# A decode kernel on one Trainium2 core: two product rows turned into columns by a matrix product instead of a trip through DRAM

## The chip, the core and the metric

The kernel runs on one core of one Trainium2 chip. The metric is the device time of one execution in microseconds (us); smaller is better. Before the change it is 402.88 us, the median of three runs (402.80, 402.88, 402.97). Beside these there is one profiled execution, on which all views of the trace rest.

## The reference, cut to what matters

One token is decoded (batch 1, sequence length 1, model width D = 1024). Its layer norm feeds two branches, whose results are added:

```python
x = A_x
xn = _layernorm(x)
return x + _A_ref(xn, A_k_cache, A_v_cache, A_wq, A_wo) + _B_ref(xn, B_w1, B_w2, B_w3, B_w4)

# _A_ref: 32 query heads, 4 key/value heads, 65536 keys of 128 values each
q = (x @ wq) ...; o = softmax(q k^T / sqrt(128)) v; return o @ wo

# _B_ref
h  = gelu(layernorm(x) @ w1)           # 1024 values
hs = concatenate([g0, g1, g2, g3]) @ w2   # g: quarters of h, each shifted along the sequence
x1 = x + hs
return x1 + gelu(layernorm(x1) @ w3) @ w4  # w3: 1024 x 3584, w4: 3584 x 1024
```

Everything is bfloat16. The sequence has one position, so each shifted quarter of `h` is a row of padding: `hs` is zero, and `x1` equals `x`. That is why the kernel can compute `layernorm(x) @ w3` early, before w1 and w2. The caches are 64 MiB each, the weights together about 34 MB; nothing is read twice.

## The kernel before, in words

**Transfers.** All large inputs go through three buffers of 64 KB per partition (tile `slot`, pool `big`, `SLOTS = 3`). The list `slots` (lines 104 to 115) gives the order: wq, K and V of the first half of key/value head 0, w3, K and V of its second half, then K and V in turn for the other heads (each transfer covers 32768 keys, 8.4 MB), with w1 and the first 13 of w4's 28 column pieces in one buffer after head 2, then wo, and last w2 with the rest of w4. `issue` (line 120) puts a load on SP's queue at line 126. A load waits until its buffer is free, so load i waits for the last reader of load i - 3, and SP issues strictly in this order.

**Attention.** `compute_K` (line 360) works on 16384 keys: VectorE transposes 32x32 blocks of K in place (line 369, eight times for each 8.4 MB load), TensorE multiplies with the query (line 373, tile `sc`), VectorE takes the maximum (377, 381, 383, 391 or 393), ScalarE the exponential (396), VectorE transposes the result into `pT` (410). `compute_V` (413) multiplies `pT` with V (420, tile `oacc`), and VectorE or ScalarE moves the result to `og` (425, 428). `group_end` (433) closes a head.

**The small layers.** `rows_product` (line 261) leaves a product with a weight matrix as rows: for w3 the 3584 results lie on partitions 0, 32, 64 and 96, in two blocks of 448 columns; the other 31 partitions of each group of 32 hold zeros, since the left operand `xpad2` has one column that is not zero. ScalarE applies the gelu (line 321, tile `hrow`; line 329, tile `h1row`). The next products, with w4 (line 348) and w2 (341), need the values as columns: `hT` with 28 values on each partition, `gT` with 8. They are used through `row_acc` (line 180), which accumulates in `psB`; only the last piece of w4 reads `psB` out and stores the result (355 to 358).

**From row to column.** `bounce` (line 310) makes the columns. GpSimd's queue (POOL) stores the rows in a DRAM scratch tensor (line 312) and, when that has landed, loads them back with the other layout (line 314, tiles `dst_h` and `dst_g`). Since all sources of `gT` are padding, `grow` is only a memset (331) and the four copies in the loop at 334 to 337 are never issued.

**What sets the order around the change.** The code is written in the order of the loads (line 476). The framework lays the instructions out on each engine: an instruction may stand ahead of one written earlier when its inputs are ready earlier, and each engine then runs its list in order. Tiles with one tag share a pool's buffers. `pT`, `psel`, `accx`, `grow` and the final `out0` share the tag "pT" with two buffers (pool `tpool`); `qrow`, `p_sb`, `hrow` and `h1row` share the tag "p" with one (`ppool`); all small PSUM tiles share the tag "pm" with two (`ps_M`). A tile waits until the earlier user of its buffer is done.

Of the kernel before, what the change touches and what calls it, by code (L numbers as in the profile page):

```python
# [8 lines left out]
BF16 = mybir.dt.bfloat16  # L9
F32 = mybir.dt.float32  # L10
ACTF = mybir.ActivationFunctionType
ALU = mybir.AluOpType
AX = mybir.AxisListType
# [11 lines left out]
def kernel(  # L25
# [14 lines left out]
    nc = tc.nc  # L40
    P = 128
# [8 lines left out]
    DC = D // P  # L50
    FC = F // P
# [9 lines left out]
    const = ctx.enter_context(tc.tile_pool(name="const", bufs=1))  # L61
    small = ctx.enter_context(tc.tile_pool(name="small", bufs=2))
    one = ctx.enter_context(tc.tile_pool(name="one", bufs=1))
    big = ctx.enter_context(tc.tile_pool(name="big", bufs=SLOTS))
    ppool = ctx.enter_context(tc.tile_pool(name="pp", bufs=1))
    tpool = ctx.enter_context(tc.tile_pool(name="tp", bufs=2))
    dram = ctx.enter_context(tc.tile_pool(name="dram", bufs=1, space=bass.MemoryType.DRAM))
    ps_S = ctx.enter_context(tc.tile_pool(name="psS", bufs=2, space=bass.MemoryType.PSUM))
    ps_O = ctx.enter_context(tc.tile_pool(name="psO", bufs=1, space=bass.MemoryType.PSUM))
    ps_M = ctx.enter_context(tc.tile_pool(name="psM", bufs=2, space=bass.MemoryType.PSUM))  # L70
# [46 lines left out]
    st = {}  # L117
# [18 lines left out]
    for a in range(4):  # L136
        nc.scalar.dma_start(out=x_bf[32 * a:32 * a + 32, :],
                            in_=A_x[0, 0, 32 * a * DC:(32 * a + 32) * DC].rearrange("(p c) -> p c", c=DC))
# [16 lines left out]
    ident_f = const.tile([P, P], F32, name="ident_f")  # L155
# [9 lines left out]
    def tmp(w):  # L165
        n_tmp[0] += w
        assert n_tmp[0] <= 512
        return early[:, n_tmp[0] - w:n_tmp[0]]
# [52 lines left out]
    for j in range(4):  # L221
# [6 lines left out]
    sel32 = tmp(32)  # L228
# [5 lines left out]
    nc.vector.tensor_tensor(out=sel8[:], in0=sel8[:], in1=sel32[:, 16:24], op=ALU.add)  # L234
    nc.vector.tensor_tensor(out=sel8[:], in0=sel8[:], in1=sel32[:, 24:32], op=ALU.add)

    maskq = const.tile([P, 4], F32, name="maskq")
    nc.vector.tensor_tensor(out=maskq[:], in0=sel8[:, 0:4], in1=sel8[:, 4:8], op=ALU.add)

# [4 lines left out]
                          in_=sel8[:].unsqueeze(2).to_broadcast([P, 8, 4]))  # L244

    selw = const.tile([P, 2], F32, name="selw")
    for b in range(2):
        nc.vector.tensor_tensor(out=selw[:, b:b + 1], in0=ident_f[:, 32 * b:32 * b + 1],
                                in1=ident_f[:, 64 + 32 * b:64 + 32 * b + 1], op=ALU.add)
# [5 lines left out]
    for b in range(2):  # L255
        for par in range(2):
            nc.vector.tensor_copy(out=psel[:, 2 * b + par, :].rearrange("p (a i) -> p a i", a=4),
                                  in_=iv[:, b, par, :].unsqueeze(1).to_broadcast([P, 4, 32]))


    def rows_product(key, part, wt, xp, width, n_chunks):
        if part == 0:
            st[key] = ps_S.tile([P, 2, 512], F32, name="rows", tag="sc")
        acc = st[key]
        n_c = wt.shape[1]
        for cl in range(n_c):
            c = n_c * part + cl
            for j in range(4):
                for bk in range(2):
                    ch = 4 * bk + j  # L270
                    if ch < n_chunks:
                        nc.tensor.matmul(acc[32 * j:32 * j + 32, bk, 0:width], lhsT=xp[:, c, :],  # L272
                                         rhs=wt[:, cl, ch * width:(ch + 1) * width],
                                         start=(c == 0), stop=(c == DC - 1), tile_position=(0, 32 * j),
                                         skip_group_check=True)
        return acc
# [30 lines left out]
                             skip_group_check=True)  # L307
        nc.vector.tensor_copy(out=qsel[:], in_=pq[:])

    def bounce(rows_ap, view, C, tag):  # L310
        scr = dram.tile([P, C], BF16, name=f"scr_{tag}")
        nc.gpsimd.dma_start(out=view(scr[:].rearrange("m c -> (m c)")), in_=rows_ap)
        dst = const.tile([P, C], BF16, name=f"dst_{tag}")
        nc.gpsimd.dma_start(out=dst[:], in_=scr[:])
        return dst

    def compute_w3():
        wt = loaded[("w3",)].rearrange("p (c n) -> p c n", n=F)
        acc = rows_product("psh", 0, wt, xpad2, FW, 8)
        hrow = ppool.tile([P, 2, FW], BF16, name="hrow", tag="p")  # L320
        nc.scalar.activation(out=hrow[:], in_=acc[:, :, 0:FW], func=ACTF.Gelu_apprx_tanh)
        st["hT"] = bounce(hrow[:].rearrange("(j u) b n -> j u b n", u=32)[:, 0],
                          lambda f: f.rearrange("(b j n) -> j b n", b=2, j=4), FC, "h")

    def compute_w1():
        wt = loaded[("w1",)].rearrange("p (c n) -> p c n", n=D)
        acc = rows_product("psh1", 0, wt, xpad2, 512, 2)
        h1row = ppool.tile([64, 512], BF16, name="h1row", tag="p")
        nc.scalar.activation(out=h1row[:], in_=acc[0:64, 0, :], func=ACTF.Gelu_apprx_tanh)
        grow = tpool.tile([64, 512], BF16, name="grow", tag="pT")  # L330
        nc.vector.memset(grow[:], 0.0)
        cq = D // 4
        for grp, shift in enumerate((1, -1, 2, -2)):
            for s in range(S):
                if 0 <= s - shift < S:
                    r0, c0 = 32 * (grp // 2), cq * (grp % 2)
                    nc.vector.tensor_copy(out=grow[r0:r0 + 1, c0:c0 + cq], in_=h1row[r0:r0 + 1, c0:c0 + cq])
        st["gT"] = bounce(grow[:].rearrange("(j u) n -> j u n", u=32)[:, 0],
                          lambda f: f.rearrange("(j n) -> j n", j=2), DC, "g")

    def compute_w2():
        wt = loaded[("w2",)].rearrange("p (c n) -> p c n", n=D)
# [125 lines left out]
    def add_wo():  # L468
        wrow = st.pop("wrow")
        for q in range(4):  # L470
            c0 = QC * (q % 2)
            row_acc(q, selw[:, q // 2:q // 2 + 1], wrow[:, c0:c0 + QC])

    compute = {"wq": compute_wq, "w3": compute_w3, "w1": compute_w1, "w2": compute_w2, "w4": compute_w4,
               "wo": compute_wo, "K": compute_K, "V": compute_V}
    for i, pieces in enumerate(slots):
# [37 lines left out]
```

## Time and profile before

| | |
|---|---|
| median of three runs | 402.88 us |
| time of the profiled execution | 402.64 us |
| its span, first to last instruction | 400.9 us |
| mean granted TensorE clock | 0.806 |
| TensorE (PE) busy | 217.9 us, 54% |
| VectorE (DVE) busy | 215.1 us, 54% |
| ScalarE (ACT) busy | 35.1 us, 9% |
| GpSimd (POOL) busy | 6.0 us, 1% |
| moved by DMA | 170.10 MB, mean 424 GB/s |

The profiled execution lies 0.24 us under the median, and 1.74 us of its time lie outside the span. "Busy" is the time in which an engine runs an instruction; a matmul's end is modelled, and matmuls overlap. The profile also names, for each group of instructions, the line, the tiles (`out<-in`), the shape, the number, the busy time and the mean time of one, and what ended the idle time before it. The chain of waits goes back from the last instruction to whatever released each step. "us to landing" is the time from a transfer's issue until its data have arrived.

### The profile page before, as it was taken

Reading aid. Unit: us, or ns where it says so; the run is one execution under the profiler, and the core shown is the slowest. Engines: PE = TensorE matmul, PEld = TensorE weight load, DVE = VectorE, ACT = ScalarE, POOL = GpSimd, SP = SyncE. Lnnn points to the kernel's source line nnn. Section 1 sums busy time; section 2 is a strip of 40 time slices with the busy share of each in tenths; the row PEclk is TensorE's granted clock in tenths of the full one; section 3 lists DMA queues with packets and bytes.
Section 4 is the critical chain, followed back from the end, with each engine's and each line's share of the span. In section 5 each row is a group of like instructions: output and inputs, shape, how many; then the busy total and the mean of one; then the engine's idle time right before and its main releaser. Section 6 shows DMA issues by size and latency. Waiting matters only on the chain.

```text
span 400.9 us, 3446 instructions
## 1 busy us (share of the span) xinstructions
PE 217.9 (54%) x1484; PEld 89.7 (22%) x1484; DVE 215.1 (54%) x249; ACT 35.1 (9%) x61; POOL 6.0 (1%) x17
## 2 busy tenths in 40 slices
PE   0006597420976396419563955486803952395773
PEld 0002232210332132104231321132401320132321
DVE  0005398401985598339846962696405962596400
ACT  0001001400012001100110011002100031002000
POOL 3000000000000000000000000000000000000000
PEclk9999879975796589958985996599765998598557
DMA  9999999999999999999999999999999999999994
GB/s 399 438 419 419 419 421 452 452 439 419 425 432 420 419 484 420 432 425 438 420 419 477 420 425 438 439 420 399 466 440 438 419 420 458 438 419 453 402 400 194
DMA packets 4088, 170.10 MB, mean 424 GB/s; under 512 B 735, under 2 KB 745, under 8 KB 1002
## 3 DMA queue, kind: packets, MB, share of 16 engines
q1 hardware_dynamic: 3752, 169.87, 98.2%
q8 instruction: 11, 0.18, 0.2%
q0 software_dynamic: 128, 0.02, 0.0%
q10 hardware_dynamic: 194, 0.00, 0.0%
q14 instruction: 3, 0.02, 0.0%
HBM read 169.88 MB, written 0.01 MB: 424 GB/s over the span
## 4 chain that ended last, share of the span: by engine, by line
DMA 51%; DVE 33%; PE 10%; another core or an unknown queue 3%; ACT 1%; issue 1%; ACTq 0%; SPq 0%; DVEq 0%
DMA slot<-in_A_k_cache_dram 37%; DVE slot L369 27%; DMA slot<-in_B_w_dram 7%; DMA x_bf<-in_A_x_dram 7%; PE oacc L420 4%; PE sc L373 3%; DVE mx L377 3%; PE rows L272 2%; DVE pT L410 1%; PE psB L181 1%; ACT p_sb L396 1%; DVE qst L285 0%; PE pm_mx L386 0%; DVE m L381 0%
## 5 line engine op out<-in xcount | busy, mean ns | idle before, releaser
L373 PE MATMUL sc<-slot,qst 128*128 128x512 bf16 x512 | 134.1, 412 | 101.2 <-DVE slot L369 101.0
L369 DVE STREAM_TRANSPOSE slot<-slot 128x2048 f32<-128x2048 f32 x64 | 142.9, 2280 | 65.7 <-DMA slot<-in_A_k_cache_dram 65.6
L373 PEld LDWEIGHTS <-qst 128*128 128x128 bf16 x512 | 51.5, 103 | 172.0 <-issue 49.5
L420 PE MATMUL oacc<-slot,pT 128*32 128x512 bf16 x512 | 43.8, 503 | 6.4 <-DVE pT L410 3.0
L396 ACT ACTIVATE p_sb<-sc,nm 128x1024 bf16<-128x1024 f32 x16 | 17.8, 1114 | 185.0 <-DVE nm L393 121.1
L410 DVE STREAM_TRANSPOSE pT<-p_sb 128x1024 bf16<-128x1024 bf16 x16 | 19.9, 1245 | 17.3 <-ACT p_sb L396 17.3
L420 PEld LDWEIGHTS <-pT 128*32 128x32 bf16 x512 | 16.0, 118 | 26.4 <-issue 16.3
L428 DVE SCALAR_TENSOR_TENSOR og<-og,alpha,oacc 128x512 f32<-128x512 f32 x12 | 9.0, 747 | 24.2 <-PE oacc L420 24.0
L377 DVE TENSOR_REDUCE mx<-sc 128x1 f32<-128x1024 f32 x16 | 19.3, 1204 | 4.5 <-PE sc L373 4.4
L193 PE MATMUL pm_ln<-early 128*128 128x1 f32 x4 | 1.1, 354 | 33.0 <-DVE early L229 30.5
L187 DVE CAST early<-x_bf 128x8 f32<-128x8 bf16 x1 | 0.2, 172 | 28.9 <-DMA x_bf<-in_A_x_dram 28.9
L379 PE MATMUL pm_mx<-ident_f,mx 128*1 128x128 f32 x16 | 4.5, 281 | 15.9 <-DVE mx L377 15.9
L396 ACT ACT_TABLE_LOAD x3 | 3.8, 1283 | 92.3 <-DVE nm L391 57.3
L443 PE MATMUL pm_e<-og,sel8q 128*32 128x128 f32 x32 | 6.0, 348 | 5.2 <-DVE og L435 5.2
L193 PEld LDWEIGHTS pm_ln<-early 128*128 128x128 f32 x4 | 1.0, 310 | 33.1 <-issue 30.5
L386 PE MATMUL pm_mx<-ident_f,rep 1*128 1x1 f32 x16 | 3.7, 229 | 8.2 <-DVE rep L383 8.2
L463 PE MATMUL pm_w<-slot,oT 128*1 128x512 bf16 x64 | 6.3, 577 | 2.2 <-DMA slot<-in_A_wo_dram 2.2
L181 PE MATMUL psB<-slot,dst_h 128*1 128x256 bf16 x112 | 5.4, 308 | 3.7 <-DMA slot<-in_B_w_dram 3.6
L272 PE MATMUL rows<-slot,xpad 128*32 128x448 bf16 (+1 forms) x80 | 5.8, 368 | 1.9 <-DMA slot<-in_B_w_dram 1.9
L386 PEld LDWEIGHTS pm_mx<-ident_f,rep 1*128 1x128 f32 x16 | 2.3, 145 | 18.4 <-DVE rep L383 18.4
L272 PE MATMUL rows<-slot,early 128*32 128x512 bf16 x64 | 6.4, 589 | 0.0
L379 PEld LDWEIGHTS pm_mx<-ident_f,mx 128*1 128x1 f32 x16 | 1.3, 79 | 21.3 <-DVE mx L377 20.4
(89 smaller groups left out, 79.9 us busy)
## 6 DMA issues: line engine op xcount, KB each, us to landing
slot<-in_B_w_dram SPq DMA_DIRECT2D x1, 7168.0 KB, 34.5
slot<-in_B_w_dram SPq DMA_DIRECT2D x2, 2048.0 KB, 26.6
slot<-in_B_w_dram SPq DMA_DIRECT2D x1, 3328.0 KB, 38.6
slot<-in_B_w_dram SPq DMA_DIRECT2D x1, 1792.0 KB, 26.0
slot<-in_B_w_dram SPq DMA_DIRECT2D x1, 1280.0 KB, 28.6
slot<-in_B_w_dram SPq DMA_DIRECT2D x1, 512.0 KB
slot<-in_B_w_dram SPq DMA_DIRECT2D x1, 256.0 KB, 29.5
slot<-in_A_k_cache_dram SPq DMA_DIRECT2D x8, 43.4
```

The costliest lines, as they stand in the source:

```text
L181: nc.tensor.matmul(psB[32 * j:32 * j + 1, :], lhsT=lhsT, rhs=rhs, start=(not row_started[j]), stop=False, tile_position=(0, 32 * j), skip_ ...
L272: nc.tensor.matmul(acc[32 * j:32 * j + 32, bk, 0:width], lhsT=xp[:, c, :], rhs=wt[:, cl, ch * width:(ch + 1) * width], start=(c == 0), sto ...
L369: nc.vector.transpose(out=kf[:, cg, :], in_=kf[:, cg, :])
L373: nc.tensor.matmul(sc[:, hf, :], lhsT=qst[:, o:o + 128], rhs=kr[:, cg, hf, :, bp // 2, :, bp % 2], start=(cg == 0 and bp == 0), stop=(cg = ...
L377: nc.vector.reduce_max(out=mx[:], in_=sc[:].rearrange("p h n -> p (h n)"), axis=AX.X)
L386: nc.tensor.transpose(pm[:, P:P + 1], rep[0:1, :], ident_f[0:1, 0:1])
L396: nc.scalar.activation(out=p_sb[:], in_=sc[:], func=ACTF.Exp, bias=nm[:, 0:1], scale=SCALE, accum_out=lb[:, 0:1])
L410: nc.vector.transpose(out=pT[:], in_=p_sb[:])
L420: nc.tensor.matmul(oacc[32 * u:32 * (u + 1), :], lhsT=pT[:, hf, 32 * t:32 * (t + 1)], rhs=vt[:, :, hf, t, :], start=(hf == 0 and t < 4), s ...
L428: nc.vector.scalar_tensor_tensor(out=st["og"][:], in0=st["og"][:], scalar=alpha[:, 0:1], in1=oacc[:], op0=ALU.mult, op1=ALU.add)
L443: nc.tensor.matmul(pe[rows, 0:P], lhsT=sel8q[:], rhs=og[:, 128 * cg:128 * (cg + 1)], start=(cg == 0), stop=(cg == 3), tile_position=(0, 32 ...
L463: nc.tensor.matmul(psW[32 * q:32 * q + 1, :], lhsT=oT[:, j:j + 1], rhs=wt[:, j, 512 * b:512 * b + 512], start=(j < 2), stop=(j >= n_j - 2) ...
```

## The change

`bounce` and its DRAM pool are gone. In its place `to_columns` does three things. A product with a matrix of ones and zeros (`spread`) copies the row that belongs to a partition onto that partition: 128 partitions x 448 values for w3 (two accumulated products, one for each block of columns), 128 x 512 for w1 (one product). A multiplication with a mask keeps the values that belong to the partition (28 of 448, or 8 of 512), and a sum over the masked blocks with a cast makes the column. The masks are made once at the start from `sel32` and `ident_f`. The `spread` matrices are filled by GpSimd memsets, nine for w3 and three for w1, and take a buffer of the tag "pT", as the masked product `colm` does.

```diff
-    dram = ctx.enter_context(tc.tile_pool(name="dram", bufs=1, space=bass.MemoryType.DRAM))
...
+    mask16 = const.tile([P, 16], F32, name="mask16")
+    nc.vector.tensor_tensor(out=mask16[:], in0=sel32[:, 0:16], in1=sel32[:, 16:32], op=ALU.add)
+    mask64 = const.tile([P, 64], F32, name="mask64")
+    nc.vector.tensor_tensor(out=mask64[:], in0=ident_f[:, 0:64], in1=ident_f[:, 64:128], op=ALU.add)
...
-    def bounce(rows_ap, view, C, tag):
-        scr = dram.tile([P, C], BF16, name=f"scr_{tag}")
-        nc.gpsimd.dma_start(out=view(scr[:].rearrange("m c -> (m c)")), in_=rows_ap)
-        dst = const.tile([P, C], BF16, name=f"dst_{tag}")
-        nc.gpsimd.dma_start(out=dst[:], in_=scr[:])
+    def to_columns(parts, mask, n_c, tag):
+        n_q = mask.shape[1]
+        pm = ps_M.tile([P, 512], F32, name="pm_col", tag="pm")
+        for i, (sel, row) in enumerate(parts):
+            nc.tensor.matmul(pm[:, 0:n_q * n_c], lhsT=sel, rhs=row, start=(i == 0), stop=(i == len(parts) - 1))
+        msk = tpool.tile([P, n_q, n_c], BF16, name="colm", tag="pT")
+        nc.vector.tensor_tensor(out=msk[:], in0=pm[:, 0:n_q * n_c].rearrange("p (q c) -> p q c", c=n_c),
+                                in1=mask[:].unsqueeze(2).to_broadcast([P, n_q, n_c]), op=ALU.mult)
+        col = one.tile([P, n_c], F32, name="colf")
+        nc.vector.tensor_reduce(out=col[:], in_=msk[:].rearrange("p q c -> p c q"), axis=AX.X, op=ALU.add)
+        dst = const.tile([P, n_c], BF16, name=f"dst_{tag}")
+        nc.vector.tensor_copy(out=dst[:], in_=col[:])
         return dst
 
     def compute_w3():
+        spread = tpool.tile([P, 2, P], BF16, name="spread_h", tag="pT")
+        nc.gpsimd.memset(spread[:], 0.0)
+        for j in range(4):
+            for b in range(2):
+                c0 = 16 * (4 * b + j)
+                nc.gpsimd.memset(spread[32 * j:32 * j + 32, b, c0:c0 + 16], 1.0)
...
-        st["hT"] = bounce(hrow[:].rearrange("(j u) b n -> j u b n", u=32)[:, 0],
-                          lambda f: f.rearrange("(b j n) -> j b n", b=2, j=4), FC, "h")
+        st["hT"] = to_columns([(spread[:, b, :], hrow[:, b, :]) for b in range(2)], mask16, FC, "h")
 
     def compute_w1():
+        spread = tpool.tile([64, P], BF16, name="spread_g", tag="pT")
+        nc.gpsimd.memset(spread[:], 0.0)
+        for j in range(2):
+            nc.gpsimd.memset(spread[32 * j:32 * j + 32, 64 * j:64 * j + 64], 1.0)
...
-        st["gT"] = bounce(grow[:].rearrange("(j u) n -> j u n", u=32)[:, 0],
-                          lambda f: f.rearrange("(j n) -> j n", j=2), DC, "g")
+        st["gT"] = to_columns([(spread[:], grow[:])], mask64, DC, "g")
```

## The prediction

> **What bounds the kernel now.** I read the page's engine and DMA rows first, then the chain of waits, then SP's timeline, then the timeline around the two steps that change. From the page:
>
> ```profile
> PE 217.9 (54%) x1484; PEld 89.7 (22%) x1484; DVE 215.1 (54%) x249; ACT 35.1 (9%) x61; POOL 6.0 (1%) x17
> ...
> DMA  9999999999999999999999999999999999999994
> ...
> q1 hardware_dynamic: 3752, 169.87, 98.2%
> ...
> q0 software_dynamic: 128, 0.02, 0.0%
> ```
>
> No engine is busy for much over half of the span, but the 16 DMA engines are at 90% or more in every slice but the last, and SP's queue (q1) alone fills 98.2%. The kernel is one unbroken stream of loads of 169.87 MB. It starts when SP issues at 0.74 us, and its last piece lands at 395.62 us by the chain of waits; what follows until 400.9 us (the last 32 products, ScalarE's copy, the store) is the only stretch with no load beside it. A change of time must lengthen or shorten the stream, open a hole in it, or touch that tail.
>
> A hole opens when SP issues a load so late that the earlier ones have all landed. SP's timeline gives the issues; two with the least in front of them, and the one behind the w1 step:
>
> ```profile
> 69.81 0.33 SPq L126 DMA_DIRECT2D slot<-in_A_k_cache_dram  x1
> ...
> 274.99 0.33 SPq L126 DMA_DIRECT2D slot<-in_A_k_cache_dram  x1
> ...
> 290.82 0.33 SPq L126 DMA_DIRECT2D slot<-in_A_k_cache_dram  x1
> ```
>
> At 69.81 us w3 is still under way; it lands at 79.48 us, when TensorE's wait for it ends. So this issue could slip 79.48 - 69.81 = 9.7 us. At 274.99 us the piece of w4 behind w1 is under way; issued near 247.1 us with 38.6 us to landing, it ends near 285.7 us: 10.7 us of cover. At 290.82 us two K and V loads stand in front: the K load lands at 305.15 us, and V needs 8.39 MB / 424 GB/s = 19.8 us more, until 324.9 us: 34 us of cover. The last issue, at 366.17 us, has wo in front of it until 383.48 us: 17 us.
>
> The trips that the change removes, from the timelines:
>
> ```profile
> 82.75 0.92 ACT L321 ACTIVATE hrow<-rows 128x896 bf16<-128x896 f32 x1 [5.73 <-PE rows L272]
> 83.97 0.74 POOL L312 DMA_DIRECT2D scr_h<-hrow  x1 [79.87 <-ACT hrow L321]
> 92.99 0.57 POOL L314 DMA_DIRECT2D dst_h<-scr_h  x1 [8.28 <-DMA scr_h<-hrow]
> 98.83 13.28 DVE L369 STREAM_TRANSPOSE slot<-slot 128x2048 f32<-128x2048 f32 x6 [20.34 <-DMA slot<-in_A_k_cache_dram]
> ...
> 282.39 0.27 DVE L331 MEMSET grow<- 64x256 uint32 x1
> 282.95 0.56 POOL L312 DMA_DIRECT2D scr_g<-grow  x1 [189.39 <-DVE grow L331]
> 293.45 0.56 POOL L314 DMA_DIRECT2D dst_g<-scr_g  x1 [9.93 <-DMA scr_g<-grow]
> 305.18 6.70 DVE L369 STREAM_TRANSPOSE slot<-slot 128x2048 f32<-128x2048 f32 x3 [15.49 <-DMA slot<-in_A_k_cache_dram]
> ```
>
> Both steps sit in a stretch in which VectorE has nothing and waits for K: 20.34 us idle before 98.83, 15.49 us before 305.18.
>
> **Removed.** Four DMAs with 8.7, 6.0, 10.2 and 9.1 us to landing, 34 us in all, and four POOL instructions (2.4 us). `dst_h` is complete near 92.99 + 6.0 = 99.0 us; the first product that reads it starts at 288.5 us. `dst_g` is complete near 302.6 us, first read at 389.4 us. Nothing waits for either, so the 34 us are worth nothing as latency. `hrow` also holds the single buffer of tag "p" until 92.7 us, but the next `p_sb` is written at 119.95 us. What can count is the DMA engines' time: q0's row rounds to 0.0%, under 0.05% x 400.9 = 0.2 us; trace records can be missing (q0 has 128 packets, as many as one of the two loads back has partitions), so I double it as a bound. Gain: 0 to 0.4 us; I take 0.15, near the printed row.
>
> [...]
>
> **Added at the start.** Two VectorE additions for the masks. The 128x32 addition at L229 takes 0.18 us, the 128x128 cast at L308 0.29 us; so 0.36 to 0.6 us. VectorE is idle from 32.35 to 34.10 us (it waits for ScalarE's L204), where they fit. If they land in the layer norm's chain instead, everything up to the issue at 69.81 slips by 0.6 us, under 9.7 us of cover: zero.
>
> **Added for w3.** Nine POOL memsets: one of 128x256 (0.30 us at L170), eight of 32x16, each between 0.09 (L158, 128x1) and 0.20 us (L160, 128x128): 1.0 to 1.9 us. They need no input but a "pT" buffer. `grow`'s memset needs no input either, and came only at 282.39 us, when the L420 batch that read an older `pT` had ended (281.6). So I take it that buffers of a tag are handed out in program order; then these memsets run from 74.73 us (end of the first L420 batch) to 76.6 us at the latest, before w3 lands (79.48). After `hrow` (83.67 us): two products 128x448 with 128x128 weights, each 0.38 to 0.63 us (fastest and slowest of L373); the multiplication 448/512 of L428 (0.747 us) or L435 (0.691), some 0.65 us; the sum between half of L377 (1.20 us for 1024 values: 0.55) and L449's rate (0.361 us for 128: 1.26); the cast 0.18 us. Together 2.1 to 3.4 us with hand-overs: done by 87.3 us. Queued behind them are L369 on VectorE and L373's first weight load on TensorE, both held by K's landing at 98.8 us. Cover 11.5 us, cost zero; if the steps were ordered into K's work instead, V's next issue at 120.05 us would slip by some 3 us, with 17 us of loads in front.
>
> **Added for w1.** Three memsets on POOL (0.3 to 0.6 us) from 281.6 us. `grow` now takes the other "pT" buffer, read by the second L420 batch until 286.05 us, so its 0.27 us memset moves behind L428 or L435 on VectorE, which has a gap of 1.15 us there. Then one product 128x512 (0.38 to 0.63), a multiplication (0.69 to 0.75), the sum (0.6 to 1.44), the cast (0.16): 1.9 to 3.0 us, done near 292 us. TensorE's new product stands ahead of the 52 products with w4's first piece that free the slot at 290.82 us, so that issue slips by up to 1.5 us, under 34 us of cover. VectorE's L446 to L452 may slip 2 us; their `oT` is read near 382 us. ScalarE and SP get nothing.
>
> [...] No row here shows POOL work beside VectorE work after 4.1 us. If the new memsets hold up VectorE at 74.7 us for their full 1.9 us, the later work at 77.75 (L428) slips, which frees no slot: the sum stays the same.
>
> **Sum.** 402.64 - 0.15 = 402.5 us for the profiled execution; the runs' median lies 0.24 us higher, so 402.7 us. Bounds of the unknowns: -0.4 us (packets) to +0.6 us (masks, if cover did not count), around 402.9: 402.5 to 403.5, with 0.3 us below for the runs' own spread (0.17 us) and the time around the span.
>
> **Rivals.** (1) *Forecast: all of it is hidden by the stream*, 402.7 us, chance 0.80.
>
> (2) *Slower: a wait on VectorE holds the slot of w1.* If `grow`'s memset were ordered behind K's eight transposes (305.18 us plus the 21.2 us that the earlier head takes from 253.77 to 274.99: 326.4 us), TensorE's new product would wait for it, and behind it the 52 products (2.3 us). SP would issue at about 329.4 instead of 290.82 us. The loads in front end at 324.9 us, so the stream stands still for 4.5 us: 407 us. It decides once the slot comes free after 324.9 us. For it: `grow`'s buffer comes free later than now. Against it: VectorE has 15 idle us before K lands, and the memset went ahead of two later instructions in this trace. Chance 0.09.
>
> (3) *Faster: the small packets or the POOL queue cost more than their own time.* To pass 0.2% (0.8 us, about what a measurement of this kernel can tell from no change), the stream must run some 2% better in the 37 us of the two trips. Against it: the table of stretches shows it no slower there:
>
> ```profile
> 84.00:99.50 15.50, 0.00 (x0) 0.10 (x1) 0.67 (x1) 0.00 (x0) 1.28 (x2) 0.54 1.03 445
> 281.50:303.00 21.50, 8.21 (x114) 4.27 (x110) 3.52 (x10) 1.87 (x2) 1.12 (x2) 0.66 1.04 448
> 98.50:281.50 183.00, 115.27 (x648) 46.16 (x648) 127.80 (x125) 15.97 (x31) 0.00 (x0) 0.80 1.00 431
> ```
>
> 445 and 448 GB/s (last column) with the trips, 431 without. Left is the 1.74 us outside the span, of which a queue less could save a part; all of it gives 401.0 us. Chance 0.11.
>
> **Numbers.** Range 402.2 to 403.5 us, the forecast's own bounds; the rivals' 0.20 lies outside. Faster 0.11, same 0.80, slower 0.09.
>
> **What would show it.** Right: q1 still fills 98%, the last landing stays within 0.4 us of 395.6, q0 is empty, the new VectorE work ends before 88 and near 292 us, and the issue at 290.82 moves by under 2 us. Wrong: a slice with DMA under 9 before the last, a K load issued after the one before it has landed, or a last landing earlier by 0.8 us or more.

## The result, and the profile after

The changed kernel takes 403.68 us (median of 11 runs, 403.56 to 404.12), the kernel before 402.80 us (median of 11 runs, 402.52 to 403.01): a ratio of 1.0022, 95% interval 1.0014 to 1.0031. The forecast was 402.7 us with a range of 402.2 to 403.5 us, so the time lies outside it, 0.18 us above its upper end, and the small gain that was expected became a loss of 0.9 us. The profiled execution took 403.74 us, its span is 402.0 us (before 400.9).

The page of the changed kernel (engine busy times, DMA share by slice, queues):

```profile
PE 215.0 (53%) x1487; PEld 89.1 (22%) x1487; DVE 218.6 (54%) x257; ACT 35.1 (9%) x61; POOL 4.9 (1%) x25
...
DMA  9999999999999999999999999999999999999994
...
q1 hardware_dynamic: 3752, 169.87, 98.1%
...
q10 hardware_dynamic: 194, 0.00, 0.0%
```

The picture is the same: SP's queue fills 98.1% of a longer span, no slice but the last is below 9, and q0 is gone with the trips. VectorE has eight instructions more.

The new steps and the three issues that the prediction watched, from the timeline of the changed kernel (its line numbers; start and duration in us):

```profile
74.84 0.31 POOL L331 MEMSET spread_h<- 128x256 bf16 x1 [70.74 <-PE oacc L441]
75.21 0.69 POOL L335 MEMSET spread_h<- 32x16 bf16 x8
82.90 0.92 ACT L339 ACTIVATE hrow<-rows 128x896 bf16<-128x896 f32 x1 [6.15 <-PE rows L275]
83.87 0.54 PE L318 MATMUL pm_col<-hrow,spread_h 128*128 128x448 bf16 x2 [1.02 <-ACT hrow L339]
84.45 0.62 DVE L320 TENSOR_TENSOR colm<-pm_col,mask 128x448 bf16<-128x448 f32 x1 [5.64 <-PE pm_col L318]
85.10 0.90 DVE L323 TENSOR_REDUCE colf<-colm 128x28 f32<-128x448 bf16 x1
86.04 0.18 DVE L325 CAST dst_h<-colf 128x28 bf16<-128x28 f32 x1
99.16 13.28 DVE L390 STREAM_TRANSPOSE slot<-slot 128x2048 f32<-128x2048 f32 x6 [12.94 <-DMA slot<-in_A_k_cache_dram]
...
288.33 0.27 DVE L353 MEMSET grow<- 64x256 uint32 x1
290.42 0.39 PE L318 MATMUL pm_col<-grow,spread_g 64*128 64x512 bf16 x1
293.10 0.17 DVE L325 CAST dst_g<-colf 128x8 bf16<-128x8 f32 x1
```

```profile
69.14 0.33 SPq L125 DMA_DIRECT2D slot<-in_A_k_cache_dram  x1
...
275.62 0.33 SPq L125 DMA_DIRECT2D slot<-in_A_k_cache_dram  x1
...
292.37 0.33 SPq L125 DMA_DIRECT2D slot<-in_A_k_cache_dram  x1
```

Everything that was added is over at 86.2 and 293.3 us; after it VectorE waits 12.94 us for K at the first place, as the bracket says, and 12.65 us at the second. The new work is not what made the kernel longer.

What did is seen where the loads land. The timeline's instructions that waited for a load, the kernel before first, then the changed one (each starts when its load has landed):

```profile
98.83 13.28 DVE L369 STREAM_TRANSPOSE slot<-slot 128x2048 f32<-128x2048 f32 x6 [20.34 <-DMA slot<-in_A_k_cache_dram]
176.39 13.28 DVE L369 STREAM_TRANSPOSE slot<-slot 128x2048 f32<-128x2048 f32 x6 [8.65 <-DMA slot<-in_A_k_cache_dram]
253.77 13.28 DVE L369 STREAM_TRANSPOSE slot<-slot 128x2048 f32<-128x2048 f32 x6 [6.21 <-DMA slot<-in_A_k_cache_dram]
344.95 13.28 DVE L369 STREAM_TRANSPOSE slot<-slot 128x2048 f32<-128x2048 f32 x6 [9.73 <-DMA slot<-in_A_k_cache_dram]
395.66 2.22 PE L181 MATMUL psB<-slot,dst_h 128*1 128x256 bf16 x32 [2.10 <-DMA slot<-in_B_w_dram]
```

```profile
99.16 13.28 DVE L390 STREAM_TRANSPOSE slot<-slot 128x2048 f32<-128x2048 f32 x6 [12.94 <-DMA slot<-in_A_k_cache_dram]
176.62 13.28 DVE L390 STREAM_TRANSPOSE slot<-slot 128x2048 f32<-128x2048 f32 x6 [7.35 <-DMA slot<-in_A_k_cache_dram]
254.42 13.28 DVE L390 STREAM_TRANSPOSE slot<-slot 128x2048 f32<-128x2048 f32 x6 [7.34 <-DMA slot<-in_A_k_cache_dram]
345.63 13.28 DVE L390 STREAM_TRANSPOSE slot<-slot 128x2048 f32<-128x2048 f32 x6 [9.80 <-DMA slot<-in_A_k_cache_dram]
396.73 2.28 PE L180 MATMUL psB<-slot,dst_h 128*1 128x256 bf16 x32 [1.76 <-DMA slot<-in_B_w_dram]
```

The lag is 0.33, 0.23, 0.65, 0.68 and 1.07 us. There is no place where it jumps: it builds up along the stream, also in stretches in which both kernels run the same instructions (0.23 us at the second of these waits, 0.65 us at the third). The tail behind the fifth wait is as long as before (402.0 - 396.73 = 5.3 us against 400.9 - 395.66 = 5.2 us). And no load came late to SP: at 69.14 us w3 was still under way until 79.62 us. The stream itself runs slower. The trace's records of the DMA packets say the same: the durations of q1's packets, summed over the 16 engines and divided by 16, are 393.6 us before and 394.2 us after; the median 64 KB packet behind the first three loads takes 2418 ns before and 2420 ns after.

### The profile page after: what moved, and what is told of

Read it like the earlier page. It is cut to its first block, busy times and chain, and to the rows that moved or that the text cites. A ratio compares the mean times of both kernels' runs of the same rounds, so it can differ in the third digit from the quotient of the medians.

```text
span 402.0 us, 3470 instructions
## 1 busy us (share of the span) xinstructions
PE 215.0 (53%) x1487; PEld 89.1 (22%) x1487; DVE 218.6 (54%) x257; ACT 35.1 (9%) x61; POOL 4.9 (1%) x25
## 3 DMA queue, kind: packets, MB, share of 16 engines
q1 hardware_dynamic: 3752, 169.87, 98.1%
## 4 chain that ended last, share of the span: by engine, by line
DMA 53%; DVE 33%; PE 8%; another core or an unknown queue 3%; ACT 2%; issue 1%; SPq 1%; ACTq 0%; DVEq 0%
DMA slot<-in_A_k_cache_dram 38%; DVE slot L390 26%; DMA slot<-in_B_w_dram 7%; DMA x_bf<-in_A_x_dram 7%; PE sc L394 3%; DVE mx L398 3%; PE oacc L441 2%; DVE pT L431 2%; PE rows L275 1%; ACT p_sb L417 1%; PE psB L180 1%; SPq L125 1%; DVE qst L288 0%; DVE m L402 0%
## 5 line engine op out<-in xcount | busy, mean ns | idle before, releaser
L394 PE MATMUL sc<-slot,qst 128*128 128x512 bf16 x512 | 136.7, 421 | 100.3 <-DVE slot L390 100.2
L390 DVE STREAM_TRANSPOSE slot<-slot 128x2048 f32<-128x2048 f32 x64 | 142.9, 2280 | 59.2 <-DMA slot<-in_A_k_cache_dram 59.2
L394 PEld LDWEIGHTS <-qst 128*128 128x128 bf16 x512 | 52.4, 104 | 172.9 <-issue 51.1
L441 PE MATMUL oacc<-slot,pT 128*32 128x512 bf16 x512 | 40.7, 474 | 5.6 <-DVE og L449 2.5
L449 DVE SCALAR_TENSOR_TENSOR og<-og,alpha,oacc 128x512 f32<-128x512 f32 x12 | 9.0, 746 | 22.0 <-PE oacc L441 21.9
L484 PE MATMUL pm_w<-slot,oT 128*1 128x512 bf16 x64 | 5.0, 479 | 5.2 <-DMA slot<-in_A_wo_dram 5.2
L464 PE MATMUL pm_e<-og,sel8q 128*32 128x128 f32 x32 | 4.2, 276 | 4.7 <-DVE og L456 4.7
L275 PE MATMUL rows<-slot,early 128*32 128x512 bf16 x64 | 5.4, 513 | 0.0
```

What stands on the lines that cost most here:

```text
L390: nc.vector.transpose(out=kf[:, cg, :], in_=kf[:, cg, :])
L394: nc.tensor.matmul(sc[:, hf, :], lhsT=qst[:, o:o + 128], rhs=kr[:, cg, hf, :, bp // 2, :, bp % 2], start=(cg == 0 and bp == 0), stop=(cg = ...
L441: nc.tensor.matmul(oacc[32 * u:32 * (u + 1), :], lhsT=pT[:, hf, 32 * t:32 * (t + 1)], rhs=vt[:, :, hf, t, :], start=(hf == 0 and t < 4), s ...
L449: nc.vector.scalar_tensor_tensor(out=st["og"][:], in0=st["og"][:], scalar=alpha[:, 0:1], in1=oacc[:], op0=ALU.mult, op1=ALU.add)
L484: nc.tensor.matmul(psW[32 * q:32 * q + 1, :], lhsT=oT[:, j:j + 1], rhs=wt[:, j, 512 * b:512 * b + 512], start=(j < 2), stop=(j >= n_j - 2) ...
```

## The experiments

Three theories were set against each other. A: the trips' small packets put the 16 DMA engines into a better rhythm, and the stream lost it with them. B: the change moved the three load buffers. The masks (64 and 256 bytes per partition) and the column tile `colf` (28 floats, which take 128 bytes) belong to pools that stand ahead of `big`, so all three buffers begin 448 bytes higher: the first at byte 26560 of the partition instead of 26112. (The addresses are those that the framework gives the tiles; no profile shows them.) C: the new work, or the issues that it shifts. My first guess was A; B was the rival. The lag that grows in stretches without a changed instruction already speaks against C.

**Before, without the trips** (this and the next three ran against a kernel before of 402.88 us):

```diff
-        scr = dram.tile([P, C], BF16, name=f"scr_{tag}")
-        nc.gpsimd.dma_start(out=view(scr[:].rearrange("m c -> (m c)")), in_=rows_ap)
         dst = const.tile([P, C], BF16, name=f"dst_{tag}")
-        nc.gpsimd.dma_start(out=dst[:], in_=scr[:])
+        nc.gpsimd.memset(dst[:], 0.0)
```

> The kernel before, without the four DMAs of the trips; the columns are two memsets of zero on POOL instead (so the products with w4 and w2 add nothing). Nothing else moves, the load buffers keep their addresses. Theory A (the trips' small packets leave the 16 DMA engines in a better rhythm for the rest of the stream; without them each 64 KB packet takes 2 ns and more longer): 403.5 to 403.8 us, with the packets' time rising after 80 us as in the changed kernel. Theory B (the change pushed the three load buffers 448 bytes up, and their new place is slower to write): 402.5 to 402.8 us. Theory C (the new work on TensorE and VectorE, or the issues that it shifts): 402.5 to 402.8 us.

Measured: 402.69 us, ratio 0.9995 (0.9986 to 1.0004). Theory A falls. The trips are worth 0.19 us as a point value, and the interval (a gain of 0.56 us to a loss of 0.16 us) does not tell that from nothing.

**Before, all from the constants on moved by 448 bytes.**

```diff
-    eps_t = const.tile([P, 1], F32, name="eps_t")
-    nc.gpsimd.memset(eps_t[:], LN_EPS)
+    eps_t = const.tile([P, 113], F32, name="eps_t")
+    nc.gpsimd.memset(eps_t[:, 0:1], LN_EPS)
```

> The kernel before, with one constant tile made 448 bytes larger, so that the load buffers and all that lie behind them stand where they stand in the changed kernel; not one instruction differs. Theory A (small packets) and theory C (new work): 402.8 us, as before. Theory B (place of the buffers): 403.5 to 403.8 us.

Measured: 404.03 us, ratio 1.0029 (1.0018 to 1.0039). The whole loss, and a little more than the 403.8 us at the upper end of what B expected, without one changed instruction. The same wait lines of this kernel:

```profile
99.28 13.28 DVE L369 STREAM_TRANSPOSE slot<-slot 128x2048 f32<-128x2048 f32 x6 [20.96 <-DMA slot<-in_A_k_cache_dram]
176.76 13.28 DVE L369 STREAM_TRANSPOSE slot<-slot 128x2048 f32<-128x2048 f32 x6 [8.48 <-DMA slot<-in_A_k_cache_dram]
254.36 13.28 DVE L369 STREAM_TRANSPOSE slot<-slot 128x2048 f32<-128x2048 f32 x6 [7.34 <-DMA slot<-in_A_k_cache_dram]
346.05 13.28 DVE L369 STREAM_TRANSPOSE slot<-slot 128x2048 f32<-128x2048 f32 x6 [10.03 <-DMA slot<-in_A_k_cache_dram]
396.96 2.27 PE L181 MATMUL psB<-slot,dst_h 128*1 128x256 bf16 x32 [2.15 <-DMA slot<-in_B_w_dram]
```

Against the kernel before the lag is 0.45, 0.37, 0.59, 1.10 and 1.30 us: the same slow growth as in the changed kernel.

**Changed, buffers in the old place.**

```diff
+    late = ctx.enter_context(tc.tile_pool(name="late", bufs=1))   # after the pool tp
...
-    mask16 = const.tile([P, 16], F32, name="mask16")
+    mask16 = late.tile([P, 16], F32, name="mask16")
-    mask64 = const.tile([P, 64], F32, name="mask64")
+    mask64 = late.tile([P, 64], F32, name="mask64")
...
-        col = one.tile([P, n_c], F32, name="colf")
+        col = late.tile([P, n_c], F32, name="colf")
```

> The changed kernel, with its two masks and the column tile in a pool behind the load buffers, so that these stand where they stood before (448 bytes lower); the instructions are the same. Theory A and theory C: 403.5 to 403.8 us, as the changed kernel. Theory B (place of the buffers): 402.5 to 402.8 us.

Measured: 402.71 us, ratio 0.9994 (0.9985 to 1.0003). With its buffers kept in place the change costs nothing that these runs can tell, so C falls. Its wait lines:

```profile
98.99 13.28 DVE L391 STREAM_TRANSPOSE slot<-slot 128x2048 f32<-128x2048 f32 x6 [12.77 <-DMA slot<-in_A_k_cache_dram]
253.81 13.28 DVE L391 STREAM_TRANSPOSE slot<-slot 128x2048 f32<-128x2048 f32 x6 [5.83 <-DMA slot<-in_A_k_cache_dram]
395.88 2.21 PE L181 MATMUL psB<-slot,dst_h 128*1 128x256 bf16 x32 [2.12 <-DMA slot<-in_B_w_dram]
```

0.16, 0.04 and 0.22 us behind the kernel before, where the changed kernel has 0.33, 0.65 and 1.07.

**Changed, with both trips made for nothing.** `scr` and the two DMAs on POOL's queue as before; what comes back goes to a tile that nothing reads.

```diff
...
+        dead_trip(hrow[:].rearrange("(j u) b n -> j u b n", u=32)[:, 0],
+                  lambda f: f.rearrange("(b j n) -> j b n", b=2, j=4), FC, "h", nc.gpsimd)
         st["hT"] = to_columns(...)
...
```

> The changed kernel, which also makes both trips through DRAM on POOL's queue as before, and reads nothing of what they bring back; the load buffers stand as in the changed kernel. Theory A (the trips' packets help the stream): 402.7 to 403.0 us. Theory B and theory C: 403.6 to 403.9 us.

Measured: 403.88 us, ratio 1.0025 (1.0016 to 1.0035). The trips repair nothing: A is out a second time.

B stands. Which tiles, and which places? Four more kernels with unchanged instructions ran against a kernel before of 402.86 us. **448 bytes between the load buffers and the tiles behind them:**

```diff
+    between = ctx.enter_context(tc.tile_pool(name="between", bufs=1))   # ahead of ppool
...
-    mask4 = const.tile([P, 4], F32, name="mask4")
+    mask4 = const.tile([P, 12], F32, name="mask4")   # takes the 32 bytes that selw leaves
...
-    selw = const.tile([P, 2], F32, name="selw")
+    selw = between.tile([P, 112], F32, name="selw")
```

> The kernel before, with 448 bytes inserted between the load buffers and the tiles behind them (p_sb, hrow, pT and their like); the load buffers stay where they stood. The instructions are the same. Theory B1 (the load buffers must begin at a multiple of some power of two; before they began at byte 26112 of the partition, 51 x 512): 402.7 to 402.9 us. Rival B2 (it is the tiles behind the buffers, such as pT, whose place matters): 403.8 to 404.1 us.

Measured: 402.86 us, ratio 0.9999 (0.9991 to 1.0008). The tiles behind the buffers don't matter in this kernel.

**The buffers up by 64 and by 256 bytes**, and later by 128 and 32, by enlarging the last tile ahead of them:

```diff
-        rl = one.tile([P, 1], F32, name="rl")
+        rl = one.tile([P, 1 + N], F32, name="rl")   # N = 16, 64, 32, 8
...
```

> The kernel before, with the last tile ahead of the load buffers 64 bytes larger: the buffers, and the tiles behind them, stand 64 bytes higher, at a multiple of 64 but not of 128. The instructions are the same. Theory B1 with a multiple of 128 or more: 403.7 to 404.1 us. B1 with a multiple of 64, or rival B3 (the sheer distance of 448 bytes matters): 402.7 to 402.9 us (448 is itself a multiple of 64, so B1 with 64 is already out by the run with 448 bytes; a fast run here would speak for B3).

Measured: 403.92 us, ratio 1.0027 (1.0017 to 1.0037). A move of 64 bytes is as bad as one of 448, so it isn't the distance.

> The kernel before, with the load buffers and the tiles behind them 256 bytes higher: a multiple of 256, not of 512. The instructions are the same. B1 with a multiple of 128 or 256: 402.7 to 402.9 us. B1 with a multiple of 512: 403.7 to 404.1 us. Where the extra time is in proportion to how far the place is off, between the two.

Measured: 402.80 us, ratio 1.0000 (0.9991 to 1.0009).

**The buffers down by 512 bytes:**

```diff
+    late = ctx.enter_context(tc.tile_pool(name="late", bufs=1))
...
-        msk = one.tile([P, 4, 32], F32, name="msk")
+        msk = late.tile([P, 4, 32], F32, name="msk")
```

> The kernel before, with the tile msk in a pool behind the load buffers: the buffers stand 512 bytes lower, again at a multiple of 512 (25600, also a multiple of 1024). The instructions are the same. B1 with a multiple up to 512: 402.6 to 402.9 us. Rival B3 (it is the distance from the old place, or an order among the tiles, and no multiple): 403.5 us or more. If a multiple of 1024 counts as well: below 402.5 us.

Measured: 402.84 us, ratio 1.0000 (0.9992 to 1.0009). A multiple of 512 or 1024 brings no more than one of 256 (402.80 us).

The next four, against a kernel before of 402.87 us, ask for 128 and for the price. **Changed, with `mask16` alone behind the buffers:**

```diff
+    late = ctx.enter_context(tc.tile_pool(name="late", bufs=1))
...
-    mask16 = const.tile([P, 16], F32, name="mask16")
+    mask16 = late.tile([P, 16], F32, name="mask16")
```

> The changed kernel, with only the 64 byte tile mask16 moved to a pool behind the load buffers: these begin at byte 26496, a multiple of 128 but not of 256. The instructions are the same. Theory D1 (a multiple of 128 is enough): 402.5 to 402.9 us, as with the buffers in the old place. Rival D2 (it takes a multiple of 256): 403.5 to 403.9 us.

Measured: 403.56 us, ratio 1.0019 (1.0011 to 1.0028). And the kernel before, up by 128:

> The kernel before, with the load buffers and the tiles behind them 128 bytes higher, a multiple of 128 and not of 256. The instructions are the same. D1 (a multiple of 128 is enough): 402.7 to 402.9 us. D2 (256): 403.7 to 404.1 us.

Measured: 403.86 us, ratio 1.0025 (1.0016 to 1.0034). Both say that 128 is not enough.

> The kernel before, with the load buffers and the tiles behind them 32 bytes higher, not even a multiple of 64. The instructions are the same. If any place off the multiple costs the same: 403.8 to 404.1 us. If a place that is off by less than 64 bytes cuts one more piece and so costs more: 404.3 us or more.

Measured: 404.17 us, ratio 1.0031 (1.0018 to 1.0043). Slower than the three other places of the kernel before off the multiple by 0.14 to 0.31 us, with intervals that overlap: a little worse than the expected flat price, and less than the 404.3 us of the other case, so it doesn't decide.

**Each buffer larger by 64 bytes:**

```diff
-        t = big.tile([P, SLOT], BF16, name="slot")
+        t = big.tile([P, SLOT + 32], BF16, name="slot")
```

> The kernel before, with each of the three load buffers 64 bytes larger, so that the middle one alone stands off a multiple of 128 (by 64); the first and the third stand on one. The instructions are the same. If each load pays for its own buffer: about a third of the 1.1 us, 403.1 to 403.4 us. If one buffer off its multiple disturbs the whole stream: 403.7 us or more. If it takes all three: 402.9 us or less.

Measured: 403.70 us, ratio 1.0020 (1.0011 to 1.0028). The expectation was written for a multiple of 128; the two runs before it show that it takes 256, and by that measure the third buffer was off too (it begins at 157312, 128 past a multiple). With two buffers of three off, 0.83 of 1.0 us is paid, so the run does not test what one buffer does. To have one off alone, **each buffer larger by 128 bytes** (`SLOT + 64`), against a kernel before of 402.91 us:

> The kernel before, with each load buffer 128 bytes larger: the buffers begin at 26112, 91776 and 157440, so only the middle one is off a multiple of 256 (by 128). It takes every third load, 31% of the bytes. If each load pays for the place of its own buffer, a third of the 1.0 us: 403.1 to 403.3 us. If one buffer off its multiple disturbs the whole stream: 403.6 us or more.

Measured: 403.22 us, ratio 1.0008 (0.9999 to 1.0017), 0.31 us more than the kernel before, where 31% of 1.0 us was expected (the loads take the first, the third and the middle buffer in turn). The interval just includes no change, and it leaves out the 1.0 us of a stream disturbed as a whole (its upper end is 0.7 us). With the run above it makes a row: one buffer off 0.31, two off 0.83, three off 0.99 us. That fits a price that each load pays for its own buffer, but does not show it. The packet records agree in part: the 14 and 10 KB packets of the last load, which goes into the middle buffer, are 3.9 and 3.5 ns longer than on a multiple where that buffer is off by 64 and the third by 128, 0.8 and 2.1 ns where it alone is off by 128, and 3.3 and 2.9 ns where all three are off by 128.

All kernels with equal remainders in one table (the buffers are 65536 bytes apart, so all three have the same remainder):

| kernel | first buffer at byte | remainder by 256 | time, us |
|---|---|---|---|
| before | 26112 | 0 | 402.88 |
| before, without the trips | 26112 | 0 | 402.69 |
| before, tiles behind moved | 26112 | 0 | 402.86 |
| before, down 512 | 25600 | 0 | 402.84 |
| before, up 256 | 26368 | 0 | 402.80 |
| changed, old place | 26112 | 0 | 402.71 |
| before, up 32 | 26144 | 32 | 404.17 |
| before, up 64 | 26176 | 64 | 403.92 |
| before, up 128 | 26240 | 128 | 403.86 |
| before, up 448 | 26560 | 192 | 404.03 |
| changed, mask16 behind | 26496 | 128 | 403.56 |
| changed | 26560 | 192 | 403.68 |
| changed, trips made for nothing | 26560 | 192 | 403.88 |

The best version tried is the changed kernel with the three tiles behind the buffers, 402.71 us. It beats the changed kernel by 0.97 us. Whether it beats the kernel before (0.9994, interval 0.9985 to 1.0003) these runs can't tell.

## Why the prediction was wrong

**The frame held.** "A change of time must lengthen or shorten the stream, open a hole in it, or touch that tail": it lengthened the stream, by 1.07 us at the last wait in the profiled pair. No hole opened, and the tail kept its length. Of the signs that were to show the forecast right, one failed, the last landing within 0.4 us of 395.6; of the signs of being wrong none appeared, because none was for a stream that runs slower without a hole.

**The step that failed is "Added at the start".** It priced the masks as two VectorE additions and asked where those fit (they ran at 30.66 and 31.84 us, 0.22 and 0.17 us, and held nothing up that counts). What the masks take is also space: 320 bytes, with `colf` 448, ahead of the load buffers. The prediction named the code's pools and never asked what stands behind a new tile. So the sum's "bounds of the unknowns: -0.4 us (packets) to +0.6 us (masks, if cover did not count)" had no term for the buffers' place, which measures 0.97 us in the changed kernel (403.68 against 402.71) and 0.99 to 1.30 us in the kernel before, with its buffers off a multiple of 256. The lengthening was looked for only in the small packets of rival 3. None of the rivals had the mechanism: the slower one, a wait that holds w1's slot, did not happen. `grow`'s memset ran at 288.33 us, between L449 and L456, and the slot's release at 292.37 us is 1.55 us later than before, of which 1.48 us stand already in the issue ahead of it (287.58 against 286.10).

**The rest of the sum was right.** With the buffers in their place the changed kernel takes 402.71 us, where the forecast said 402.7 (the small gain itself is not clear of the noise):

- Removed: "Gain: 0 to 0.4 us; I take 0.15". The run without the trips gives 0.19 us, not clear of nothing.
- Added for w3: POOL's nine memsets ran from 74.84 to 75.90 us (expected 74.73 to 76.6 at the latest), the two products overlapped and took 0.54 us together (0.76 to 1.26), the multiplication 0.62 (0.65), the sum 0.90 (0.55 to 1.26), the cast 0.18. Done at 86.2 us, before the 87.3 us that were allowed.
- Added for w1: 0.39, 0.69, 1.06 and 0.17 us, done at 293.3 us (near 292). The new memsets did not hold VectorE up: the L449 that ran beside w1's memsets, at 283.14 us, took 0.75 us, as L428 did before (747 ns on average).
- The range's lower part and the time around the span were right as well: 403.74 - 402.0 = 1.74 us, the same as before, so a queue less saves nothing there.

One reading was wrong, without weight for the sum: 395.62 us is not the landing of the stream's last piece. It is the last that TensorE's chain waited for; by the packet records q1 moves two smaller pieces of w4 after it, until 397.1 us (398.1 us in the changed kernel, 1.0 us later).

**How the place costs time.** What is shown is that the buffers' place sets the time; how it does so is open in part. The packets' own records point to a price for each packet that hardly depends on its size between 10 and 64 KB. In the changed kernel, the 64 KB packets behind the first three loads are 3 ns longer on average than in the six kernels on a multiple of 256 (before, without the trips, tiles behind moved, down 512, up 256, changed in the old place), those of 26, 16, 14 and 10 KB 3.7 to 4.7 ns, those of 4 and 2 KB 1.9 and 1.1 ns. Spread evenly, 1.0 us over q1's 3328 packets of 2 KB or more, 208 for each of the 16 engines if they share them alike, would be 4.8 ns for a packet (an estimate). The remainder counts for little: of the 64 KB packets behind the first three loads, 3 to 12% took longer than 2418 ns on a multiple of 256, 73 to 74% with a remainder of 128, 73 to 92% with 64 or 192, and 98% with 32.

Summed over the engines and divided by 16, q1's durations come to 393.5 to 393.8 us in the six kernels on a multiple of 256 and to 394.1 to 394.5 us in those with all three buffers off it; 393.7 us for one buffer off and 393.9 us for two can hardly be told from the first group. That is 0.6 to 0.7 us of the 1.0; the rest is not in these durations. Slower reading of the moved buffers by VectorE is not what is seen: its transposes in `slot` take 2280 ns on average before and after, and the packets of the last load are longer while VectorE has nothing to do (0.00 us busy from 384 to 396 us). What is not explained: the packets of the first three loads are no longer in any kernel (median 2418 ns before and in the changed one), and those of w3 hardly (0.3 to 2.6 ns), though their buffers are as far off. So by these records a packet's price does not hang on its own place alone.

What the runs show is the multiple of 256, for loads that write into SBUF: 64, 128 and 448 bytes up take 403.92, 403.86 and 404.03 us, 256 up and 512 down 402.80 and 402.84 us. The price is not seen to grow with the remainder: 404.17 us for 32, 404.03 us for 192. Why it is 256, no run shows.

## What to carry to other kernels

Where a stream of loads is the bound, a new tile can cost its place too, as it did here (0.97 us): look at what stands behind it, and try the load buffers at a multiple of 256 bytes (put small tiles behind them, or fill up ahead of them), which took 402.7 to 402.9 us here against 403.6 to 404.2 us off it. To allocate them first would not do by itself: in this program the first tile stands, by the framework's addresses, at byte 16512, 128 past a multiple, and a remainder of 128 took 403.56 and 403.86 us. A difference of a few tenths of a per cent that grows along the run, with the same waits and no hole, may be in none of the changed steps; move tiles without touching an instruction before explaining it by the instructions. Off-path work beside a stream that fills the DMA engines cost nothing measurable here (402.71 us with the buffers in their place, 402.88 us before), as reckoned, and neither did the trip that it replaced (402.69 us without it).

## What the runs showed of the hardware that was not expected

- The place within the SBUF partition at which the load buffers begin changes the time of a stream of 8.4 MB loads (64 KB for each partition): with all three at a multiple of 256 bytes the kernel takes 402.7 to 402.9 us, with all three off it (by 32, 64, 128 or 192) 403.6 to 404.2 us, 0.2 to 0.3% more. By the packet records of the changed kernel, those of 64 KB take 3 ns longer and those of 26 to 10 KB 3.7 to 4.7 ns.
- The four small DMAs of the trips through DRAM (6.0 to 10.2 us each to landing) and POOL's queue cost the stream 0.19 us as measured, not clear of nothing, and the time outside the span nothing (1.74 us in the profiled executions before and after).
